# Moving the scaling and the sums of two weight groups in a fused state-space and mish kernel

## The chip, the cores and the metric

The kernel runs on one core of a Trainium2 chip. The core has five engines with an instruction queue each: PE (TensorE, matrix products), DVE (VectorE), ACT (ScalarE), POOL (GpSimd) and SP (SyncE, here only an issuer of DMAs). Each queue is worked off in order, and an instruction that waits for a semaphore holds up everything behind it on its queue. The metric is the device time of one execution in microseconds (us); less is better. Three executions of the kernel before took 611.64, 612.21 and 613.2 us, so the median is 612.21 us.

## The reference: what is computed

The input x has 2048 tokens of 1024 features. Each token is normalised, `xn = layernorm(x)`, and two layers are added to x:

```python
out = x + A(xn) + B(xn)
# A: a diagonal complex recurrence over the 2048 tokens
Bu  = xn @ B_bar.T                      # 1024 -> 1024 complex
h_t = Lam_bar * h_{t-1} + Bu_t          # one state per feature, token after token
y   = 2 * Re(h @ C.T) + xn * Dskip      # 1024 complex -> 1024
# B: a dense layer with the mish activation
u   = xn @ w1 + b1                      # 1024 -> 3584
act = u * tanh(softplus(u))
z   = act @ w2                          # 3584 -> 1024
```

## The kernel before, in words

The tokens go through in four blocks of 512 (`blk` 0 to 3). The code counts from zero, so "block 2" of the change is `blk == 1`, which the code calls `FAST`, and "weight groups six and seven" are the groups 5 and 6 below. A block has these stages on PE: the first layer of B (28 tiles of 128 of the 3584 columns, `first_tile`, weights of w1 through a ring of 7 slots), the projection into the states (B_bar), then the `tail`: the second layer of B (28 tiles, 8 PSUM banks as accumulators) and the projection out of the states (C), which adds into the same banks. While PE is in the tail's dense part, DVE runs the recurrence: `recur(blk, j)` for j = 0 to 7, two scans and four products and sums each. At the end `finish` adds the banks to x on DVE, a quarter of the tokens at a time, and ACT issues the stores.

From `blk` 1 on, the projection into the states is made with seven products of half size in place of eight, from sums of the weights and sums of xnT ("1" to "7" of pairs a to d in the orders `HEAD` and `WHOLE`; L882 are its matmuls; `evacuate` copies or adds what they leave in PSUM, on DVE for a and b, and for c and d on ACT with the additions on DVE). In `blk` 2 and 3 (`SPLIT`) the first layer of B is made in the same way (L952).

For that, the 1024 x 3584 matrix w1 must be turned into scaled 16-bit sums once, in seven groups of 512 columns, while blocks 0 and 1 run. For group i:

- `w_load(i)`: four DMAs on POOL's queue (L1026, 256 KB each) bring the group into SBUF. There are only three places: groups 0, 3 and 5 share one in the tile `hb`, groups 1, 4 and 6 share the other in `hb`, and group 2 lies in `act`. A load waits until the last sums of the group before it in its place have been stored.
- a power of two per group: for groups 3 to 6 from maxima taken in block 0; for groups 0 to 2 from `w_abs(i)` (a sum of absolute values, ACT, L1037), `w_row(1)` (POOL, two small DMAs through DRAM so that every partition sees every value, L1060 and L1063) and `w_exponent(1)` (seven small DVE instructions, L1071 to L1078).
- `w_scale(i)`: two ACT instructions (L1087) that scale the group in place, then three POOL DMAs (L1081) that store the raw units 1, 2 and 4 to the DRAM tensor `wsd`.
- `w_sums(i)`: four DVE instructions (L1102), which write units 5, 7, 6 and 3 over the group's own place, so that each but one waits for a store of `w_scale` to have landed; each is followed by one POOL store. With `later=True` the four are only put on the list `steps`, and the mark `k0` in an order, or `steps.pop(0)()`, takes the next one from it.

The places of all this are written by hand. In `blk` 1, `side(f)` puts work behind tile f of the first layer; `project_fast` walks through `WHOLE`, in which `v` is `w_scale`, `n` is `w_load`, `u` opens a unit of the tail (six dense matmuls), `r` is `rotate_in` on DVE; the loop over `recur` places the rest. Before the change: group 5 is scaled behind tile 20 and summed behind tile 26; group 6 is loaded behind tile 23, scaled at the head of the projection (`v6`) and summed at its four `k0`; groups 0 and 1 are loaded at the projection's end (`n0 n1`) and group 2 behind `recur(1)`; groups 0 to 2 are scaled behind `recur(6)`, and their twelve sums are steps in the first projection of `blk` 2.

Of the kernel before, what the change touches and what calls it, by code (L numbers as in the profile page):

```python
# [163 lines left out]
def build_kernel(nc, A_x, A_Lambda_re, A_Lambda_im, A_B_re, A_B_im, A_C_re, A_C_im,  # L164
# [16 lines left out]
    FAST = 1  # L181
# [1 line left out]
    SPLIT = range(2, NB)  # L183
    GROUPS = ((0, 7), (7, NPL), (NPL, NPL + 8), (NPL + 8, NF))
    HEAD = "a2 a1 b2 b1 a5 b5 a6 b6 a3 b3 a7 b7 c2 d2 a4 b4 c5 c1 r0 d5 d1 r1 c6 c3 d6"
    HEAD1 = "v6 " + HEAD.replace("a4 b4 c5 c1 r0 d5 d1 r1", "a4 k0 b4 c5 c1 k0 r0 d5 d1 k0 r1 k0")
    WHOLE = HEAD1 + " d3 c7 d7 u7 c4 r2 u5 d4 u6 u4 r3 n0 n1 r4 r5 r6 r7"
    LATE = (" a3 b3 a7 b7 c2 d2 a4 b4 c5 c1 d5 d1 c6 c3 d6"
            " d3 c7 w1 d7 w5 w2 c4 d4 w6 r0 x1 x5 x2 w7 w3 r1 x6 w4 y1 y5 y2 x7 x3 r2 y6 x4"
            " z1 z5 g2 z2 y7 y3 z6 y4 u0 z7 u2 z3 u1 z4 u7 g3 r3 r4 r5 r6 r7")  # L190
# [162 lines left out]
    ncs, _ = early("ncs", [P, NR], f32, 10752)  # L353
# [665 lines left out]
    def w_load(i):  # L1019
        sem = DmaSem(nc, "d_wraw%d" % i, nper=4)  # L1020
        for ci in range(2):
            for kh in range(2):
                dst, b_dst = w_unit(w_raw(i, ci, kh))
                f0 = (4 * i + 2 * ci) * P
                src = B_w1[kh * NH * P:(kh + 1) * NH * P, f0:f0 + 2 * P].rearrange("(k p) f -> p k f", p=P)
                PO.dma(lambda e, dst=dst, src=src: e.dma_start(dst.rearrange("p (k f) -> p k f", k=NH), src),  # L1026
                       sem, writes=b_dst)
# [56 lines left out]
    def w_scale(i):  # L1084
        for ci in range(2):
            t, b_t = w_half(i, ci)
            aop(lambda e, t=t: e.activation(t, t, AF.Copy, scale=wsm(2, i, i + 1)),  # L1087
                reads=b_t + [b_wsm[2][i]], writes=b_t)
        for n, ci, kh in ((1, 0, 0), (2, 0, 1), (4, 1, 1)):
            w_store(i, n, *w_unit(w_raw(i, ci, kh)))  # L1090

    steps = []

    def w_sums(i, later=False):
        (rl_, b_rl_), (rh_, b_rh_), (il_, b_il_), (ih_, b_ih_) = (w_unit(w_raw(i, ci, kh))
                                                                  for ci in range(2) for kh in range(2))
        for n, o, b_o, x, b_x, y, b_y, op in ((5, ih_, b_ih_, il_, b_il_, ih_, b_ih_, ALU.add),
                                              (7, il_, b_il_, rl_, b_rl_, il_, b_il_, ALU.subtract),
                                              (6, rl_, b_rl_, ih_.bitcast(f16), b_ih_, rl_, b_rl_, ALU.subtract),
                                              (3, rh_, b_rh_, rh_, b_rh_, rl_.bitcast(f16), b_rl_, ALU.subtract)):  # L1100
            def step(n=n, o=o, b_o=b_o, x=x, b_x=b_x, y=y, b_y=b_y, op=op):
                vop(lambda e: e.tensor_tensor(o.bitcast(f16), x, y, op=op), reads=b_x + b_y, writes=b_o)  # L1102
                w_store(i, n, o, b_o)

            steps.append(step)
        while steps and not later:
            steps.pop(0)()
# [282 lines left out]
    for blk in range(NB):  # L1390

        def side(f):
            if blk:
                at = (8, 10, 12, 15)
                if f in at:
                    ln_skip(blk, at.index(f))
                    if blk >= FAST:
                        sums_x(at.index(f))
                if blk == FAST:
                    if f == 1:  # L1400
                        rows_spread(1)
                    if f == 0:
                        scale_B(0, (1,))
                    if f < 3:
                        scale_B(f + 1)
                    if f in (3, 4, 17, 19):
                        sums_B((3, 4, 17, 19).index(f))
                    if f in (2, 14, 20):
                        w_scale((2, 14, 20).index(f) + 3)
                    if f in (6, 8, 10, 12):  # L1410
                        rows_C(f // 2 + 1)
                    if f == 12:
                        snaps_ready()
                    if f in (10, 19, 26):
                        w_sums((10, 19, 26).index(f) + 3)
                    if f in (15, 23):
                        w_load((f - 15) // 8 + 5)
                    if f == 27:
                        w_sums(6, True)
                return  # L1420
            if f == 2:
                turn_sines()
            if f == NR:
                aop(lambda e: e.activation(act[:, 0:NR, 0:2 * P], hraw[:, 0:NR, :], AF.Mish),
                    reads=b_hbf[0:4], writes=b_actf[0:NR])
            if f in (19, 27):
                for j in range(4):
                    table(j + (4 if f > 19 else 0))
            if f in (5, 6, 7, 8):
                coefficients(f - 5)  # L1430
            if f in (8, 9, 11, 12):
                ln_skip(0, (8, 9, 11, 12).index(f))
            if f in turns:
                transpose_B(turns.index(f))
            if f >= 26:
                transpose_C(f - 26)
            if f >= 4 * ROWS[0][0] and f % 4 < 2:
                w_most(f // 4, f % 4)
            if f in (23, 25, 26, 27):
                ln_stats_only(1, (23, 25, 26, 27).index(f))  # L1440
            if f == 26:
                w_row(0)

        for f in range(0 if blk in SPLIT else NF):
            first_tile(blk, f)
            side(f)

        near = 0 < blk < NB - 1
        out_stage = tail(blk, n_item[0] + (len(W_ITEMS) if blk in SPLIT else 0))
        open_unit = next(out_stage)  # L1450
        if blk in SPLIT:
            if near:
                for q in range(NQ):
                    load_x(PO, blk + 1, q)
            project_fast(blk, STEPS if near else SEVEN, open_unit)
        elif blk:
            project_fast(blk, WHOLE, open_unit)
        else:
            project_in()
        if near and blk not in SPLIT:  # L1460
            for q in range(NQ):
                next_stats(blk + 1, q)
            w_abs(0)
            w_abs(1)
        for j in range(NJ):
            if blk == 0 and j == NJ - 1:
                rows_scale(0)
            recur(blk, j)
            if near and j == (5 if blk in SPLIT else 1):
                next_root()  # L1470
                for q in range(NQ):
                    next_scale(blk + 1, q)
            if blk in SPLIT:
                if j == 1:
                    next(out_stage)
                if near and j == 1:
                    for q in range(NQ):
                        next_stats(blk + 1, q)
                if near and j == 5:
                    for q in range(NQ):  # L1480
                        transpose_dma(q)
                continue
            if blk:
                if j == 1:
                    next(out_stage)
                    w_load(2)
                    w_abs(2)
                    w_row(1)
                if j == 6:
                    w_exponent(1)  # L1490
                    for i in (0, 1, 2):
                        w_scale(i)
                continue
            if j == 0:
                ln_root()
                w_exponent(0)
                for q in range(NQ):
                    ln_scale(1, q)
                next(out_stage)
                for i in range(NHS):  # L1500
                    rows_load(i)
            scale_C(j)
            for i in {4: (0, 1, 2), 5: (3, 4, 5, 6), 6: (7, 8, 9, 10), 7: range(11, 16)}.get(j, ()):
                rows_size(i)
        if near:
            for q in range(NQ):
                ln_skip(blk + 1, q)
            for n in range(4):
                sums_x(n, VE)
        if blk < NB - 1:  # L1510
            carry()
        if blk == FAST:
            for i in (0, 1, 2):
                w_sums(i, True)
        if blk == FAST - 1:
            w_load(3)
            rows_scale(1)
            vop(lambda e: e.tensor_tensor(qi[:], qi[:], c("ss").unsqueeze(1).to_broadcast([P, 2, NJ]), op=ALU.mult),
                reads=[b_qi] + b_ss, writes=[b_qi])
            rows_spread(0)  # L1520
            scale_B(0, (0,))
            for j in range(4):
                rows_C(j)
            w_load(4)
        for _ in out_stage:
            pass
# [36 lines left out]
```

## Time and profile before

| what | value |
|---|---|
| profiled execution: time | 612.28 us |
| its span | 611.0 us |
| median of three executions | 612.21 us (611.64 to 613.2) |
| PE busy | 598.2 us, 98% of the span |
| DVE busy | 476.4 us, 78% |
| ACT busy | 278.4 us, 46% |
| POOL busy | 123.2 us, 20% |
| mean granted PE clock | 0.997 of full |

The span is what the profiler saw from the first to the last instruction; the time has 1.3 us more around it. "L1102" is line 1102 of the kernel before. A start such as 218.61 is in us from the start of the span. In a timeline a line gives start, length, engine, line, operation, what is written and read, how many instructions were merged, and in brackets how long the engine sat idle before it and what ended that. A matmul of 512 columns shows as 379 ns and one of 256 as 273 ns because neighbours overlap; from start to start they take 216 and 109 ns, so one product of eight half-size matmuls takes 0.874 us (eight products begin between 225.26 and 232.25). "PEclk" in a table of windows is the granted PE clock as a share of full speed.

### The profile page before, as it was taken

What the parts mean: (1) busy time and instruction counts of PE and PEld (TensorE: products, weight loads), DVE (VectorE), ACT (ScalarE), POOL (GpSimd) and SP (SyncE); (2) the same over time, 40 slices, a digit from 0 to 9 for tenths busy, and PEclk for the clock granted to TensorE, in tenths of its full rate; (3) what the DMA queues carried; (4) which work ended last, traced back from release to release, by engine and by line L of the source; (5) the groups of instructions that cost most, each with busy time, mean ns of one, the idle gap of its engine ahead of it and who ended that gap; (6) DMA issues with size and microseconds to landing.
All of it is one profiled execution on the core that took longest, in us unless ns stands there. A gap on an engine that the chain in (4) does not pass through costs nothing.

```text
span 611.0 us, 9307 instructions
## 1 busy us (share of the span) xinstructions
PE 598.2 (98%) x3583; PEld 349.2 (57%) x3583; DVE 476.4 (78%) x748; ACT 278.4 (46%) x367; POOL 123.2 (20%) x162
## 2 busy tenths in 40 slices
PE   9999999999999879999999999999999999999998
PEld 7644444444444457444448888644446888744444
DVE  6997899999789467989936877699943577689923
ACT  4749605489488432891706516570304615620000
POOL 2899200322338432500302200000000000000000
PEclk9999999999999989999999999999999999999999
DMA  9999998992999971969769917654666805754521
GB/s 235 318 228 278 205 178 230 268 352 50 267 362 337 342 260 71 280 202 220 254 201 375 375 41 239 208 205 138 182 198 240 281 15 167 248 206 142 165 73 69
DMA packets 109670, 132.95 MB, mean 218 GB/s; under 512 B 54346, under 2 KB 69322, under 8 KB 109626
## 3 DMA queue, kind: packets, MB, share of 16 engines
q1 hardware_dynamic: 97168, 95.77, 53.9%
q0 software_dynamic: 8768, 28.26, 14.0%
q10 hardware_dynamic: 3690, 8.34, 4.0%
q8 instruction: 28, 0.46, 0.3%
q14 instruction: 16, 0.13, 0.1%
HBM read 99.04 MB, written 21.24 MB: 197 GB/s over the span
## 4 chain that ended last, share of the span: by engine, by line
PE 70%; DVE 17%; DMA 7%; ACT 2%; issue 2%; POOL 1%; ACTq 0%; DVEq 0%; SPq 0%
PE ps L1193 37%; PE ps L952 10%; PE ps L882 9%; PE ps L818 6%; PE ps L1139 5%; DVE hT L1158 3%; DMA wsd<-hb 2%; DVE CT L789 2%; DVE CT L786 2%; DVE mt L1163 2%; ACT snaps L972 2%; DMA ring<-in_B_w_dram 1%; DMA scd<-sbf 1%; DMA hb<-in_B_w_dram 1%; DVE hb L1102 1%
## 5 line engine op out<-in xcount | busy, mean ns | idle before, releaser
L1193 PE MATMUL ps<-ring,act 128*128 128x512 bf16 x896 | 195.7, 379 | 0.4 <-DMA ring<-in_B_w_dram 0.3
L1193 PEld LDWEIGHTS ps<-ring,act 128*128 128x128 bf16 x896 | 87.6, 98 | 104.2 <-DMA ring<-in_B_w_dram 1.4
L972 ACT ACTIVATE snaps<-ps,par,cs 128x256 f32<-128x256 f32 x80 | 43.4, 563 | 99.0 <-PE ps L952 49.4
L818 PE MATMUL ps<-xnT,ring 128*128 128x512 bf16 x392 | 84.9, 379 | 0.0
L1193 PE MATMUL ps<-ring,hT 128*128 128x512 bf16 x378 | 82.1, 379 | 0.0
L818 PEld LDWEIGHTS ps<-xnT,ring 128*128 128x128 bf16 x392 | 38.3, 98 | 46.1
L1193 PEld LDWEIGHTS ps<-ring,hT 128*128 128x128 bf16 x378 | 36.9, 98 | 44.7
L1158 DVE TENSOR_TENSOR_SCAN hT<-cs,qi,hT 128x512 bf16<-128x512 f32 x48 | 58.9, 1269 | 0.0
L952 PE MATMUL ps<-TT,ring 128*128 128x256 f16 x448 | 55.8, 273 | 0.5 <-ACT snaps L972 0.5
L989 DVE SCALAR_TENSOR_TENSOR act<-ps,cs,snaps 128x512 bf16<-128x512 f32 x42 | 31.4, 750 | 31.2 <-PE ps L952 26.2
L952 PEld LDWEIGHTS ps<-TT,ring 128*128 128x128 f16 (+1 forms) x448 | 43.7, 98 | 6.9 <-issue 1.0
L952 PE MATMUL ps<-xnT,ring 128*128 128x256 bf16 x336 | 42.9, 273 | 0.0
L1163 DVE TENSOR_TENSOR mt<-hT,tab 128x1024 bf16<-128x1024 bf16 x64 | 41.4, 688 | 1.1
L1262 DVE TENSOR_TENSOR xx<-ps,xx 128x1024 bf16<-128x1024 f32 (+1 forms) x16 | 18.8, 1190 | 28.8 <-PE ps L1193 28.7
L826 ACT ACTIVATE act<-ps,par 128x512 bf16<-128x512 f32 (+1 forms) x56 | 33.6, 666 | 12.8 <-PE ps L818 10.9
L1087 ACT ACTIVATE hb<-hb,cs 128x2048 bf16<-128x2048 bf16 x12 | 23.3, 1995 | 32.3 <-DMA hb<-in_B_w_dram 16.7
L952 PEld LDWEIGHTS ps<-xnT,ring 128*128 128x128 bf16 (+1 forms) x336 | 32.9, 98 | 4.7
L841 ACT ACTIVATE act<-act 128x4096 bf16<-128x4096 bf16 (+2 forms) x8 | 25.5, 3189 | 19.0 <-DVE act L975 19.0
L1081 POOL DMA_DIRECT2D wsd<-hb x42 | 23.0, 550 | 49.3 <-DVE hb L1102 23.6
L848 DVE TENSOR_TENSOR mt<-hT,tab 128x1024 bf16<-128x1024 f16 x48 | 31.0, 687 | 0.4
L882 PE MATMUL ps<-TT,SS 128*128 128x256 f16 x192 | 24.9, 283 | 4.0 <-DVE snaps L897 4.0
L1102 DVE TENSOR_TENSOR hb<-hb 128x1024 f16<-128x1024 bf16 (+1 forms) x24 | 18.4, 767 | 13.4 <-DMA wsd<-hb 13.1
(178 smaller groups left out, 810.2 us busy)
## 6 DMA issues: line engine op xcount, KB each, us to landing
ring<-in_B_w_dram SPq DMA_DIRECT2D x84, 512.0 KB, 5.0
ring<-wsd SPq DMA_DIRECT2D x98, 256.0 KB, 4.1
ring<-ctd SPq DMA_DIRECT2D x24, 512.0 KB, 3.4
wsd<-hb POOLq DMA_DIRECT2D x42, 256.0 KB, 6.2
hb<-in_B_w_dram POOLq DMA_DIRECT2D x24, 256.0 KB, 5.9
ctd<-act ACTq DMA_DIRECT2D x8, 512.0 KB, 5.9
out_dram<-xx ACTq DMA_DIRECT2D x15, 256.0 KB, 3.4
xx<-in_A_x_dram POOLq DMA_DIRECT2D x12, 256.0 KB, 6.8
```

Of the source, the lines that this page charges most:

```text
L818: PE.mm(lambda e, k=k, w=w: e.matmul(ps[:, bank, :], lhsT=w, rhs=xnT[:, k, :], start=k == 0, stop=k == NK - 1), reads=[b_ring[s]] + b_xnT, ...
L826: aop(lambda e: e.activation(at[0][:, ts], ps[:, bank, ts], AF.Mish, bias=b1(f)), reads=[b_ps[bank], b_par], writes=[at[1]])
L841: aop(lambda e: e.activation(t, t, AF.Mish), reads=b, writes=b)
L848: vop(lambda e, s=s: e.tensor_tensor(mt[:, s, :, :], hT16[:, :, j, :], tab[:, s, j, :].unsqueeze(1).to_broadcast([P, 2, TB]), op=ALU.mult) ...
L882: PE.mm(lambda e, w=w, x=x, o=o, begin=begin, end=end: e.matmul(ps[:, bank, o:o + TH], lhsT=w, rhs=x, start=opens and begin, stop=end, ski ...
L952: PE.mm(lambda e, w=w, x=x, o=o, begin=begin, end=end: e.matmul(ps[:, bank, o:o + TH], lhsT=w, rhs=x, start=opens and begin, stop=end, ski ...
L972: aop(lambda e, o=o, p=p, j=j: e.activation(o, p, AF.Identity, scale=ig, bias=b1(f0 + j)), reads=[b_ps[b], b_par, b_ig], writes=b_dst)
L989: vop(lambda e: e.scalar_tensor_tensor(out=dst, in0=bank(b), scalar=ig, in1=src, op0=ALU.mult, op1=ALU.add), reads=[b_ps[b], b_snap[k], b_ ...
L1139: PE.mm(lambda e, j=j, ci=ci, k=k, bank=bank: e.matmul(ps[:, bank + ci, :], lhsT=BT[:, ci, j, k, :], rhs=xnT[:, k, :], start=k == 0, stop= ...
L1158: vop(lambda e, ci=ci, init=init: e.tensor_tensor_scan(out=hT[:, ci, j, :], data0=cj("r", j).to_broadcast([P, TB]), data1=hT[:, ci, j, :], ...
L1163: vop(lambda e, s=s: e.tensor_tensor(mt[:, s, :, :], hT[:, :, j, :], tab[:, s, j, :].unsqueeze(1).to_broadcast([P, 2, TB]), op=ALU.mult), ...
L1193: PE.mm(lambda e: e.matmul(ps[:, u, :], lhsT=lhsT, rhs=rhs, start=st_, stop=last), reads=reads, writes=[b_ps[u]], first=st_, last=last, te ...
```

## The change

Group 5 is no longer scaled and summed inside the first layer of `blk` 1: it is scaled at the head of the projection, behind ACT's last mish, and summed at the projection's four `k0`, the first of which moves one product later. Group 6 is loaded at the head of the projection behind group 5's raw stores, scaled behind d6 (ACT's last snapshot), and summed behind `recur(0)` and `recur(1)`, two sums each. The load of group 1, which needs group 6's place, moves behind them, its `w_abs` behind the next block's normalisation, and the exponents and scalings of groups 0 to 2 from behind `recur(6)` to behind `recur(7)`. PE's and SP's instructions and their order stay as they are, and the number of instructions on every engine too.

```diff
-    HEAD1 = "v6 " + HEAD.replace("a4 b4 c5 c1 r0 d5 d1 r1", "a4 k0 b4 c5 c1 k0 r0 d5 d1 k0 r1 k0")
-    WHOLE = HEAD1 + " d3 c7 d7 u7 c4 r2 u5 d4 u6 u4 r3 n0 n1 r4 r5 r6 r7"
+    HEAD1 = "v5 n6 " + HEAD.replace("a4 b4 c5 c1 r0 d5 d1 r1", "a4 b4 k0 c5 c1 k0 r0 d5 d1 k0 r1 k0")
+    WHOLE = HEAD1 + " v6 d3 c7 d7 u7 c4 r2 u5 d4 u6 u4 r3 n0 r4 r5 r6 r7"
...
-                    if f in (2, 14, 20):
-                        w_scale((2, 14, 20).index(f) + 3)
+                    if f in (2, 14):
+                        w_scale((2, 14).index(f) + 3)
...
-                    if f in (10, 19, 26):
-                        w_sums((10, 19, 26).index(f) + 3)
-                    if f in (15, 23):
-                        w_load((f - 15) // 8 + 5)
+                    if f in (10, 19):
+                        w_sums((10, 19).index(f) + 3)
+                    if f == 15:
+                        w_load(5)
                     if f == 27:
-                        w_sums(6, True)
+                        w_sums(5, True)
...
             w_abs(0)
-            w_abs(1)
+            w_sums(6, True)
         for j in range(NJ):
             if blk == 0 and j == NJ - 1:
                 rows_scale(0)
             recur(blk, j)
+            if blk == FAST and j < 2:
+                for _ in range(2):
+                    steps.pop(0)()
+                if j == 1:
+                    w_load(1)
...
                     w_load(2)
+                    w_abs(1)
                     w_abs(2)
                     w_row(1)
-                if j == 6:
+                if j == 7:
                     w_exponent(1)
                     for i in (0, 1, 2):
                         w_scale(i)
```

## The prediction, made before the result was known

> **What bounds the kernel now.** I read the page first, then who waits for whom on PE, then the windows and timelines of the two places where PE is not full.
>
> ```profile
> PE 598.2 (98%) x3583; PEld 349.2 (57%) x3583; DVE 476.4 (78%) x748; ACT 278.4 (46%) x367; POOL 123.2 (20%) x162
> ...
> PE ps L882 <- DVE snaps L897: 4.0, 1, 4.0
> PE ps L882 <- ACT act L826: 2.6, 2, 2.2
> PE ps L882 <- DVE hT L907: 1.3, 1, 1.3
> ```
>
> PE is busy for 98% of the span, so only what PE waits for, or loses in clock, can be won; what other engines do is worth nothing by itself. The three waits below the dots are all that PE has between 160 and 260 us, and they lie in one stage: the projection of `blk` 1. The timelines of PE, ACT, DVE and POOL there, and the windows behind them, say whose they are.
>
> ```profile
> 167.72 42.25 PE L818 MATMUL ps<-xnT,ring 128*128 128x512 bf16 x195
> 212.13 1.91 PE L882 MATMUL ps<-xnT,BT 128*128 128x256 bf16 x16 [2.16 <-ACT act L826]
> 214.44 1.91 PE L882 MATMUL ps<-xnT,BT 128*128 128x256 bf16 x16 [0.41 <-ACT act L826]
> 216.19 1.91 PE L882 MATMUL ps<-TT,SS 128*128 128x256 f16 x16
> 222.14 3.28 PE L882 MATMUL ps<-TT,SS 128*128 128x256 f16 x16 [4.05 <-DVE snaps L897]
> 225.26 1.91 PE L882 MATMUL ps<-xnT,SS 128*128 128x256 bf16 x16
> ...
> 207.52 3.90 ACT L1087 ACTIVATE hb<-hb,cs 128x2048 bf16<-128x2048 bf16 x2 [8.90 <-DMA hb<-in_B_w_dram]
> 211.32 4.14 ACT L826 ACTIVATE act<-ps,par 128x512 bf16<-128x512 f32 x7
> 223.25 3.90 ACT L1087 ACTIVATE hb<-hb,cs 128x2048 bf16<-128x2048 bf16 x2 [7.79 <-DMA hb<-in_B_w_dram]
> ...
> 218.61 2.87 DVE L1102 TENSOR_TENSOR hb<-hb 128x1024 f16<-128x1024 bf16 x4 [13.09 <-DMA wsd<-hb]
> ...
> 222.00:226.00 4.00, 3.86 (x23) 2.95 (x24) 3.93 (x8) 2.75 (x2) 0.78 (x2) 0.63 0.45 170
> ...
> 290.72 0.42 DVE L1168 TENSOR_TENSOR hT<-mt 128x512 bf16<-128x512 bf16 x1
> 291.06 0.66 DVE L1071 TENSOR_REDUCE cs<-wmx 128x3 f32<-128x384 f32 x1
> ...
> 312.63 1.23 DVE L1262 TENSOR_TENSOR xx<-ps,xx 128x1024 bf16<-128x1024 f32 x1 [6.18 <-PE ps L1193]
> ```
>
> ACT stands at 198.6 before group 5's scaling, because its load has not landed; behind it seven mishes queue up, PE runs through its eight banks and waits for the first of them. DVE stands from 205.5 before group 5's sums, because a raw store has not landed; behind it are the snapshots of a1 and b1, which free the banks that a6 and b6 write. After its idle time PE's granted clock is 0.63 in the window from 222 to 226. The last two rows are for later: DVE reaches the exponents with no wait, and has 6 us left before PE needs it again.
>
> **What the change takes away.** The first layer ends at 209.97 in the model of ends; its last matmul began at 209.59 and takes 0.216 from start to start, so the projection could begin at 209.81. Six products before a6 at 0.874 make 5.24, so a6 could begin at 215.05; it begins at 222.14: **7.09 us** of waiting (2.16 + 0.41 + 4.05, and 0.16 of overlap lost at each). Then a6 and b6 take 3.12 (225.26 less 222.14) where two products take 1.75: **1.37 us** of low clock. Together 8.46. With group 5 behind the last mish no ACT instruction waits in front of a mish, and DVE, idle from 205.5, takes a1's snapshot when a1 ends. It has 14 instructions of about 0.65 for the first 16 products of 0.874, so it keeps up. Both waits and the clock loss go: **-8.46**.
>
> **What is late next, step by step** (new times are old ones less 8.46 from a3 on, so c5 begins at 223.8 instead of 232.25).
>
> Group 5's scaling, 2 ACT instructions of 1.99: last mish until 210.8, scaling until 214.7 (load landed at 207.5). Behind it ACT has c5's snapshot, wanted at 224.7. Cost 0, covered by 10 us. Its third store (unit 4), which the first sum needs: in the old run DVE could go on 7.2 us after ACT's scaling ended (211.42 to 218.61), so now at 221.9. The first `k0` follows b4's cast, on DVE at 224.8. Cover 2.9; with the slowest of these stores (8.4 to landing, issued at 215.0) 223.4, still in time. The four sums cost what group 6's cost there before, DVE's time 2.7 either way, and the first now falls into 1.35 us in which DVE waited for a snapshot. PE's third wait, 1.3 us for c7's addition, comes from the DVE chain behind it, which does not change: it stays. Cost 0.
>
> Group 6's load, 4 POOL DMAs behind group 5's three stores: issue from 215.7, landing as before 11.8 after the end of group 5's scaling (211.4 to 223.25), so 226.5. Its scaling stands behind d6's snapshot, which ends at 230.95: cover 4.4. It holds ACT until 234.85; behind it is c4's cast, wanted at 236.4 (244.84 before), which PE's unit u4 waits for. Cover 1.5, cost 0; each us beyond would be a us of PE.
>
> Group 0's load (`n0`): POOL now holds it until group 5's last sum, at 232.8, is stored: about 240.5 instead of 243.23, landing near 249. `w_abs(0)` on ACT is reached at 250.7. Cost 0.
>
> Group 6's sums, 4 DVE instructions and 4 POOL stores behind two scans: +2.7 on DVE, but the wait of 2.4 before L551 goes, since `w_abs(1)` no longer stands before it on ACT. DVE ends `recur(7)` at about 287.4 (297.2 less 8.46, less the 1.7 of exponents now behind it, +0.3). PE needs j = 7 only in `finish`, from about 301. Cost 0.
>
> Groups 1 and 2, then the exponents: the long chain. Group 6's last sum at 260.1, its store landed near 266.5 (6.2 is the median); eight loads of 0.75 on POOL, the last until 272.5, landed near 279; `w_abs(1)` and `w_abs(2)` until 283.6; the two small DMAs took 11 us from the end of `w_abs(2)` (276.9) to about 288: now 294.6. DVE stands 7 us before L1071. From there to the end of the carry it needs 10.9 (306.5 less 291.06, without `recur(7)`'s 4.5): 305.5. `finish` wants DVE at 304.2, 306.8, 309.4 and 311.9, 1.23 each, so the first is 1.3 late and the third in time. The stores and PE's first product of `blk` 2 (from 311.7) see nothing. Behind L1076, ACT scales groups 0 to 2, six instructions, until 307.8, still before its stores of x; their nine POOL stores end at 309 and delay the next loads of x by 1 us. The sums of group 0 begin 3.5 us into `blk` 2, when its stores landed 8 us earlier. SP's order is the same; its loads of units of groups 5 and 6 come later than 300, and these stores land by 267. Cost 0, with 2.7 us of cover: PE is held only if the row lands after 297.3 (its landing + 10.9 + four finishes of 1.24 against 313.2).
>
> **Sum.** 612.28 of the profiled execution less 8.46 is **603.8** (span 602.5). The profiled execution is 0.07 above the median, so it stands for the median too.
>
> **A rule that speaks against the change.** Eight loads were issued from POOL in 5.95 us from 243.23 on, 0.744 each, while DVE was busy without a break; four took 2.99 at 212.24 while DVE stood idle. So busy DVE costs POOL's issue nothing here. The Trainium skill, "SBUF — State Buffer", section "SBUF: two separate sides", says that a two-port DVE instruction locks GpSimd out, so that it cannot write the descriptors of its DMAs; by that rule the loads moved between scans would be starved, and the sum would be that of rival 3; this trace so far disagrees.
>
> **Rivals.** (1) Part of it comes back at the projection: a store or load of groups 5 or 6 lands later than any seen, DVE waits at a `k0` or ACT before c4's cast. For: cover of only 2.9 and 1.5 us. Against: the slowest landing seen still fits. If the store takes 11.3, the longest landing of any on `wsd`, DVE is 1.5 to 2 late: 605.5. (2) The chain to the exponents is slow at every step: 8.4 for the store, 8.7 for the load, 5.4 twice for the rows. Then the row lands at 299.2, PE stands 1.9: 605.7. (3) Slower than before: POOL's issues wait behind scans. Each of the 14 between group 6's sums and the second small DMA then loses up to one scan, 1.27: the row lands at 312, PE stands 15 us, 619. It decides from a row at 305.8 on, 11 us later than worked out; speaking against it are the eight issues above. (4) The waits are not group 5's, and others take their places at once (mishes still late, snapshots still late): 611 to 612.5. Against: ACT's and DVE's rows name the load and the store.
>
> **Numbers.** Forecast 0.74; rivals 1 and 2 together 0.13; rival 3 0.05; rival 4 0.08, of which half within 0.3% (1.8 us, about what a measurement of this kernel can tell from no change) and half somewhat faster. A gain above 8.46 has no source but chip to chip differences of the size of the three executions (1.5 us). Range 602.4 to 607.3: the forecast, both bounds of rivals 1 and 2, and 1.5 beside. Faster by over 0.3%: 0.91; within: 0.04; slower: 0.05.
>
> **What will show it.** PE's first projection group starts at about 209.8 with no wait for ACT's mishes, a6 at about 215 at granted clock 1.00; the sums of group 5 begin near 224.8 without a wait for a DMA; the 1.3 before c4 is still there; DVE stands some 7 us before the exponents' first instruction, now behind `recur(7)`, and PE does not see it. Wrong it would be if PE waited at the start of `blk` 2, or DVE at the first `k0`.

## The result, and the profile after

The changed kernel takes 609.21 us (median of five executions, 607.7 to 609.85) against 613.2 us for the kernel before on the same chip (five executions, 611.64 to 613.86). The ratio is 0.9935 with a 95% interval of 0.9912 to 0.9958: 4.0 us faster, where 8.5 were forecast, and outside the forecast range (602.4 to 607.3). The profiled execution took 609.85 (span 608.6), 2.43 under the one before; it is the slowest of the five.

The first half of the prediction came out to about a tenth of a microsecond. These lines of the changed kernel answer to those shown of before: waits of PE over the whole span, then timelines of PE, ACT and DVE around the projection of `blk` 1.

```profile
PE ps L952 <- DVE xx L1262: 3.1, 1, 3.1
PE ps L1193 <- DMA ring<-in_B_w_dram: 1.1, 2, 0.7
...
195.67 14.19 PE L818 MATMUL ps<-xnT,ring 128*128 128x512 bf16 x64
209.70 3.66 PE L882 MATMUL ps<-xnT,BT 128*128 128x256 bf16 x32
...
235.18 1.05 PE L882 MATMUL ps<-TT,BT 128*128 128x256 f16 x8 [1.31 <-DVE hT L907]
...
210.48 3.88 ACT L1087 ACTIVATE hb<-hb,cs 128x2048 bf16<-128x2048 bf16 x2
...
224.48 0.68 DVE L1102 TENSOR_TENSOR hb<-hb 128x1024 f16<-128x1024 bf16 x1
```

PE goes from the first layer into the projection at 209.70, and the waits for ACT's mishes and for a6 are gone from the list. The granted clock stays at 1.00 from 208 to 233. These are lines of PE in the kernel before, at c4 and at the start of `blk` 2:

```profile
243.76 1.05 PE L882 MATMUL ps<-TT,BT 128*128 128x256 f16 x8 [1.32 <-DVE hT L907]
...
320.20 1.04 PE L952 MATMUL ps<-xnT,ring 128*128 128x256 bf16 x8
...
327.57 1.91 PE L952 MATMUL ps<-TT,ring 128*128 128x256 f16 x16 [0.23 <-ACT snaps L972]
```

The product c4, which began at 243.76, begins at 235.18: **8.58 us** won. The wait of 1.3 before c4 is still there. New on top of the list is a wait of 3.1 for DVE's `finish` (L1262) at the start of `blk` 2. The next lines are the timelines of ACT, POOL, DVE and PE of the changed kernel on the way there, and one of its windows, in which the last three columns are the granted clock, the share of the DMA engines and GB/s.

```profile
275.99 3.62 ACT L1037 ACTIVATE CT<-hb 128x4096 bf16<-128x4096 bf16 x1 [11.07 <-DMA hb<-in_B_w_dram]
286.54 3.62 ACT L1037 ACTIVATE CT<-act 128x4096 bf16<-128x4096 bf16 x1 [6.84 <-DMA act<-in_B_w_dram]
...
318.92 6.42 ACT L972 ACTIVATE snaps<-ps,par,cs 128x256 f32<-128x256 f32 x12 [3.40 <-DVE xx L1262]
...
265.46 2.23 POOL L1026 DMA_DIRECT2D hb<-in_B_w_dram  x3 [1.97 <-DMA wsd<-hb]
267.69 2.96 POOL L1026 DMA_DIRECT2D act<-in_B_w_dram  x4
290.54 0.56 POOL L1060 DMA_DIRECT2D wmd<-cs  x1 [19.89 <-ACT CT L1037]
...
286.78 0.42 DVE L1168 TENSOR_TENSOR hT<-mt 128x512 bf16<-128x512 bf16 x1
302.53 0.67 DVE L1071 TENSOR_REDUCE cs<-wmx 128x3 f32<-128x384 f32 x1 [15.34 <-DMA wmx<-wmd]
313.50 4.61 DVE L1262 TENSOR_TENSOR xx<-ps,xx 128x1024 bf16<-128x1024 f32 x4
...
314.86 1.03 PE L952 MATMUL ps<-xnT,ring 128*128 128x256 bf16 x8 [3.09 <-DVE xx L1262]
...
324.43 1.91 PE L952 MATMUL ps<-TT,ring 128*128 128x256 f16 x16 [0.76 <-ACT snaps L972]
...
315.50:318.60 3.10, 3.10 (x18) 2.21 (x17) 2.60 (x3) 0.01 (x1) 0.54 (x1) 0.55 1.02 378
```

Group 2's load is issued from 267.69 to 270.65 and `w_abs(2)` gets it at 286.54. The row of maxima lands at 302.5, DVE has stood 15.3 us before it, and its four `finish` instructions run from 313.50 instead of from 304. PE could have begun `blk` 2 at 311.6 (304.70 + 7.07, less the 0.16 of overlap) and begins at 314.86, and then runs at a granted clock of 0.55 for three microseconds.

The loss counted: from where PE could begin to its first product that waits for ACT's snapshots, the kernel before needs 7.37 us (320.20 to 327.57), the changed one 12.82 (311.61 to 324.43), so 5.45 of the 8.59 that had reached this place are lost. What sets this is the last of the four `finish`: it ends at 318.1, ACT's snapshots stand on ACT's queue behind the store that follows it, the first begins at 318.92, and PE's product comes 5.51 later. With load 2 first (below), where PE waits for no `finish` and the clock is full, that stretch is 5.52 long (312.78 to 318.30). So PE's wait of 3.1 and its low clock lie inside the 5.45 and add nothing to it. That leaves 3.14. Another 0.9 goes at the next opening of dense units, where PE waits 1.1 for ring loads instead of 0.3; 2.2 are left there, and the two profiled spans differ by 2.4 at their ends.

### The profile page after: what moved, and what is told of

The parts are those of the page before. It is cut to its first block, busy times and chain, and to the rows that moved or that the text cites. A ratio compares the mean times of both kernels' runs of the same rounds, so it can differ in the third digit from the quotient of the medians.

```text
span 608.6 us, 9262 instructions
## 1 busy us (share of the span) xinstructions
PE 595.7 (98%) x3541; PEld 348.8 (57%) x3583; DVE 475.4 (78%) x748; ACT 278.5 (46%) x367; POOL 122.8 (20%) x162
## 4 chain that ended last, share of the span: by engine, by line
PE 78%; DVE 9%; DMA 5%; issue 5%; ACT 2%; POOL 1%; SPq 1%; ACTq 0%; DVEq 0%; POOLq 0%
PE ps L1193 37%; PE ps L818 14%; PE ps L952 11%; PE ps L882 10%; PE ps L1139 5%; DMA ring<-in_B_w_dram 2%; DVE mt L848 2%; ACT snaps L972 2%; DMA wmd<-cs 1%; PE ps L638 1%; DVE xx L1262 1%; DVE hT L907 1%; DVE hT L1158 1%; DMA wmx<-wmd 1%; DMA wsd<-hb 1%
## 5 line engine op out<-in xcount | busy, mean ns | idle before, releaser
L1262 DVE TENSOR_TENSOR xx<-ps,xx 128x1024 bf16<-128x1024 f32 (+1 forms) x16 | 18.5, 1186 | 18.7 <-PE ps L1193 18.6
L897 DVE COPY snaps<-ps 128x512 f32<-128x512 f32 x30 | 19.9, 685 | 12.9 <-PE ps L882 12.8
L907 DVE TENSOR_TENSOR hT<-ps,snaps 128x512 f16<-128x512 f32 x36 | 24.4, 689 | 5.6 <-PE ps L882 3.7
```

Of the source, the lines that this page charges most:

```text
L907: vop(lambda e: e.tensor_tensor(dst, bank(b), src, op=ALU.add), reads=[b_ps[b], b_src], writes=b_hT[ci][j0:j0 + 2])
```

## The experiments

Theory 1: PE pays for the late row of maxima. Group 2's load stands on POOL behind group 6's stores, then moves beside the DMA transposes of the next block's xn; the row comes late, and DVE, which waits for it ahead of `finish`, is late with it. Theory 2, the rival: the loss comes from the DMA traffic of that stretch as such (C rows or transposes late), and DVE's wait only happens to lie beside it. Each time below is a median; a ratio is to the kernel before on the same chip, with its 95% interval, and a difference in us is worked out from the ratio.

**Group 2's load first.** POOL's order around `recur(1)` is changed, and the order of two `w_abs`; group 6's last two sums move with their stores, behind the normalisation's two small instructions on DVE:

```diff
-            if blk == FAST and j < 2:
+            if blk == FAST and j == 0:
                 for _ in range(2):
                     steps.pop(0)()
-                if j == 1:
-                    w_load(1)
...
                     w_load(2)
-                    w_abs(1)
+                    for _ in range(2):
+                        steps.pop(0)()
+                    w_load(1)
                     w_abs(2)
+                    w_abs(1)
                     w_row(1)
```

> Edit: the changed kernel, but behind recur(1) the load of group 2 is issued from POOL ahead of group 6's last two sums' stores and of group 1's load, and w_abs(2) ahead of w_abs(1). Theory 1 (the row of maxima is late because group 2's load stands on POOL behind group 6's stores and then moves beside the transposes of the next block): load 2 is issued from about 255 and landed by 265, the row lands near 292, DVE is through before finish wants it at 304.2, PE starts blk 2 with no wait at full clock: 8.5 us under the kernel before, 4.5 under the changed one. Theory 2 (the loss at the start of blk 2 is due to DMA traffic as such, the C rows or the transposes being late, and not to the row): the same bytes move in the same stretch, so it stays within 1 us of the changed kernel, 3 to 4.5 us under the kernel before.

Measured: 603.55 us against 613.05, ratio 0.9852 (0.9837 to 0.9867): 9.1 us under the kernel before. Timelines of ACT, POOL, DVE and PE:

```profile
264.85 3.62 ACT L1037 ACTIVATE CT<-act 128x4096 bf16<-128x4096 bf16 x1 [1.93 <-DMA act<-in_B_w_dram]
277.23 3.62 ACT L1037 ACTIVATE CT<-hb 128x4096 bf16<-128x4096 bf16 x1 [8.68 <-DMA hb<-in_B_w_dram]
...
312.78 6.49 ACT L972 ACTIVATE snaps<-ps,par,cs 128x256 f32<-128x256 f32 x12 [9.47 <-DVE xx L1262]
...
254.59 2.98 POOL L1026 DMA_DIRECT2D act<-in_B_w_dram  x4
...
290.32 0.67 DVE L1071 TENSOR_REDUCE cs<-wmx 128x3 f32<-128x384 f32 x1 [3.77 <-DMA wmx<-wmd]
303.35 1.23 DVE L1262 TENSOR_TENSOR xx<-ps,xx 128x1024 bf16<-128x1024 f32 x1 [1.97 <-PE ps L1193]
...
310.92 1.04 PE L952 MATMUL ps<-xnT,ring 128*128 128x256 bf16 x8
...
318.30 1.91 PE L952 MATMUL ps<-TT,ring 128*128 128x256 f16 x16 [0.23 <-ACT snaps L972]
```

Load 2 is in use at 264.85, the row lands at 290.3, DVE waits for PE at `finish` and not the other way, and PE enters `blk` 2 with no wait. Theory 1 expected 8.5, theory 2 at most 4.5. The ratio of this version is 0.0083 below that of the changed kernel, 5 us. No version below is faster, and two of them cannot be told from it (0.9853 and 0.9858).

**No wait for the row.** The two small DMAs and everything before them stay, DVE does not use their result:

```diff
-        vop(lambda e: e.tensor_reduce(out=m, in_=src.rearrange("p (q j) -> p j q", j=n),
-                                      axis=mybir.AxisListType.X, op=ALU.max), reads=b_wmx[h], writes=b_m)
+        if h == 1:
+            vop(lambda e: e.tensor_scalar(m, wsm(1, 3, 6), 1.0, None, op0=ALU.mult), reads=b_wsm[1][3:6], writes=b_m)
+        else:
+            vop(lambda e: e.tensor_reduce(...))
```

> Edit: the changed kernel, but the exponents of groups 0 to 2 are worked out from the maxima of groups 3 to 5, which DVE has had since block 0 (the loads, w_abs and the two small DMAs of the row all stay, only their result is not used: this part of the computation, the own maxima of groups 0 to 2, is left out). So DVE waits for nothing at the exponents. Theory 1: DVE goes on at 287.4, is through by 298, PE starts blk 2 at once: 8.5 us under the kernel before. Theory 2: PE still waits or slows at the start of blk 2 with the DMA traffic unchanged: 4 us under the kernel before.

Measured: 604.53 against 613.05, ratio 0.9863 (0.985 to 0.9877), 8.4 us less. The loads were as late as in the changed kernel (`w_abs(2)` began at 287.5), the DMA share from 262 to 292 was 1.05 as there, and PE began `blk` 2 with no wait:

```profile
311.75 1.04 PE L952 MATMUL ps<-xnT,ring 128*128 128x256 bf16 x8
```

So the loss comes by the wait for the row. What the late traffic may cost PE beside it is at most the 0.7 us between this version and the one with load 2 first, and the intervals of the two overlap. Theory 2 falls.

**The wait behind the carry, and behind recur(6).** Two places for the same wait. In the first, `w_exponent(1)` and the three `w_scale` are moved from behind `recur(7)` to behind `carry()`; in the second, to where they were before the change (this edit is shown):

```diff
-                if j == 7:
+                if j == 6:
                     w_exponent(1)
                     for i in (0, 1, 2):
                         w_scale(i)
```

> Edit: the changed kernel with the exponents and the scaling of groups 0 to 2 behind the carry, so that DVE does the skip terms, the sums of x and the carry before it waits for the row. Theory 1: the row lands at 302.5 as in the changed kernel, DVE is ready for the first finish at 304.2, so PE sees no wait for DVE; but ACT scales from 304 to 315.6 and its first snapshot of blk 2 comes at 316.3 where 313.6 would be free: about 2.7 us of the 8.5 are lost, so 5.8 us under the kernel before and 1.5 to 2 under the changed one. Theory 2: no change against the changed kernel (4 us under the kernel before).

> Edit: the changed kernel with one part undone: the exponents and the scaling of groups 0 to 2 behind recur(6) again, as before the change. Theory 1: the row lands near 302.5 all the same, now recur(7), 4.5 us, stands behind the wait too, and everything up to finish comes 4.5 us later: about 4.5 us slower than the changed kernel, within 1 us of the kernel before. Theory 2 (DVE's wait for the row is not what PE pays): within 1 us of the changed kernel, since PE wants the last scan only from about 301 on.

Measured: behind the carry 606.9, ratio 0.9907 (0.9891 to 0.9923), 5.7 us under the kernel before; behind `recur(6)` 613.31, ratio 1.001 (0.9995 to 1.0026), nothing left of the gain. In the first, DVE waits until 302.65 with all other work done and is at `finish` at 304.31; now ACT's scalings end at 315.6 and its first snapshot comes at 315.54, so PE waits 2.5 for snapshots in all, against 0.5 in the kernel with load 2 first, near the 2.7 worked out (its profiled execution of 609.1 us also waits 2.4 for units of `wsd`, so not all of its loss is the snapshots). In the second, PE waits for the results of the last `recur` themselves:

```profile
PE ps L1193 <- DVE hT L1166: 4.5, 1, 4.5
```

Against load 2 first, one row that lands near 302 costs about 3 us (behind the carry), 5 (the changed kernel) or 10 (behind `recur(6)`), by what stands behind the wait.

**Why the load was late.** Theory C: the transposes on SP stretch it. Theory D: eight loads in a row are slow by themselves. In the first of two kernels only SP's transposes move (`f1 = 21` in place of 17 in `blk` 1), which puts two of SP's plain loads of C ahead of them. In the second it is POOL's order, load 2 ahead of load 1 and both behind group 6's last store, and with it the order of the two `w_abs`.

> Edit: the changed kernel, but in blk 1 SP issues the four transposes of the next block's xn behind dense tiles 21 to 27 in place of 17 to 23, about 7 us later; POOL's order is untouched. Theory C (the transposes, which move through the same 16 DMA engines, are what stretches group 2's load from some 7 to 16 us): the eight loads of 262 to 271 land before or soon after the transposes begin at about 274, load 2 by about 278, w_abs(2) ends near 284, the row lands near 297, PE loses at most 1 us at the start of blk 2: 7.5 to 8.5 us under the kernel before. Theory D (eight loads in a row on POOL are slow by themselves): load 2 lands at 286 as in the changed kernel, the row at 302, and the time stays within 1 us of the changed kernel's.

> Edit: the changed kernel with the loads of groups 1 and 2 exchanged on POOL's queue, both still behind group 6's last store, and w_abs(2) ahead of w_abs(1). Load 2 need not wait for the landing of these stores, so it goes at 261 to 264 and load 1 at 264 to 267, the last of the eight 3.5 us sooner than in the changed kernel and just ahead of the first transpose at 267. Theory C: most of the eight pass before the transposes, load 1 lands near 279, the row near 293: no wait at blk 2, about 8.5 us under the kernel before. Theory D: eight loads take 23 us from the first to the last landing, so load 1 lands near 284, the row near 299.5: PE loses 2 us, 6 to 6.5 us under the kernel before.

Measured: transposes later 604.41 against 612.78, ratio 0.9858 (0.984 to 0.9875), 8.7 us less, with the row at 295.1; loads exchanged 604.19, ratio 0.9853 (0.9832 to 0.9874), 9.0 less. First the DMA issues of the changed kernel between 262 and 292 (size, median from issue to landing), then windows of it; then the same of the kernel with the later transposes.

```profile
act<-in_B_w_dram POOLq DMA_DIRECT2D x4, 256.0 KB, 13.9
xnT<-xn SPq DMA_TRANSPOSE x4, 11.4
...
271.00:275.00 4.00, 4.00 (x20) 1.84 (x19) 3.93 (x7) 0.00 (x0) 0.00 (x0) 1.00 1.16 140
275.00:279.00 4.00, 3.95 (x19) 1.78 (x19) 3.93 (x6) 3.01 (x1) 0.00 (x0) 1.00 1.25 121
```

```profile
act<-in_B_w_dram POOLq DMA_DIRECT2D x4, 256.0 KB, 7.1
xnT<-xn SPq DMA_TRANSPOSE x4, 6.0
...
271.00:275.00 4.00, 4.00 (x21) 1.80 (x19) 3.93 (x6) 0.00 (x0) 0.00 (x0) 1.00 0.94 295
275.00:279.00 4.00, 4.00 (x20) 1.82 (x19) 3.93 (x7) 3.71 (x2) 0.00 (x0) 1.00 1.37 335
```

With the same eight loads issued at nearly the same times, but the transposes from 274.8 on, load 2 lands in 7.1 instead of 13.9 us (longest 11.1 instead of 16.6), and a transpose in 6.0 instead of 11.4. From 271 to 279 the changed kernel, with loads and transposes in flight, reads as fully busy on its DMA engines and moves 140 and 121 GB/s; the version with later transposes moves 295 before the first of them, and 335 beside it and the last loads; over 271 to 283 it is 145 against 277 GB/s. So moving the transposes is enough to bring the loads back in time: theory C holds for the changed kernel. Theory D is out, since eight loads in a row landed soon enough.

Transposes beside loads are not slow in every case, though. In the exchanged version the last of the eight loads was issued by 267.96 instead of 270.65, about when the first transpose went out (267.87); its loads landed in 4.6 to 9.5 us, `w_abs(1)` began at 276.8 and the row came at 290.4. With load 2 first, only group 1's four loads (issued from 266.05 to 269.43) met the transposes (from 266.7 on), and they landed in at most 8.5. The long landings came only where loads issued behind the first transpose met four others still in flight; which of the two counts for how much is not shown. What inside the DMA engines makes them slow each other is not shown.

The Trainium skill, "DMA: Bandwidth & Descriptors", section "Issuing engines are not separate DMA queues", says that transfers from all issuers run on the same 16 engines and interleave. These rows agree: SP's transposes and POOL's loads slow each other in the changed kernel although they are issued from different queues.

**One stall alone.** Into the kernel before, only group 5's sums are moved out of DVE's queue behind tile 26, and the projection gets eight marks:

```diff
-"a4 k0 b4 c5 c1 k0 r0 d5 d1 k0 r1 k0"
+"a4 k0 k0 b4 c5 c1 k0 k0 r0 d5 d1 k0 k0 r1 k0 k0"
...
+                    if f == 26:
+                        w_sums(5, True)
```

> Edit: the kernel before with one part of the change alone: group 5's sums are taken from behind tile 26 and put on the list, and the projection has eight marks in place of four, two at each place, for the sums of groups 5 and 6. ACT's scalings, all loads and the tail stay as they were. Expected if the two stalls are separate and as sized in the prediction: the 4.05 of waiting for DVE (with its lost overlap 4.2) and the 1.37 of low clock go, ACT's 2.9 stays; the four further sums stand in the DVE chain that PE waits for ahead of c4, three of them not covered, about 1.9, so PE's wait there grows from 1.3 to about 3.2. Sum: 3.7 us under the kernel before. If the waits were one and the same (rival 4 of the prediction): within 1 us of the kernel before.

Measured: 609.87 against 612.78, ratio 0.9945 (0.9925 to 0.9966), 3.4 us less (3.7 expected). Timeline of PE:

```profile
212.01 1.91 PE L882 MATMUL ps<-xnT,BT 128*128 128x256 bf16 x16 [1.57 <-ACT act L826]
...
240.23 1.89 PE L882 MATMUL ps<-TT,BT 128*128 128x256 f16 x8 [3.41 <-DVE hT L907]
```

ACT's waits stay and DVE's at a6 is gone: they are two stalls. The wait before c4 grows from 1.3 to 3.4 (3.2 expected), which is a reason for the change to take group 6's four sums out of the projection when it puts group 5's in. In this execution (610.9 us) c4 begins 3.53 earlier than before (240.23 against 243.76), but behind that wait the clock was 0.50 from 240 to 243, which the expectation had left out, and at PE's next product of the projection only 2.19 are left (243.75 against 245.94). So it is in part luck that the measured 3.4 comes so near to 3.7; its interval is 2.1 to 4.6.

**Control.** The changed kernel again, beside the last three.

> The changed kernel once more beside these, as a control: 4 us under the kernel before, the row of maxima landing near 302 by the trace.

Measured: 609.37 against 612.78, ratio 0.9929 (0.991 to 0.9948), 4.4 us less, with the row at 302.8 and PE's wait of 3.0 at `blk` 2.

## Why the prediction was right and wrong

- *What the change takes away, -8.46:* right; 8.58 at c4. Both waits and the low clock went, and with the stall on DVE alone taken away 3.53 were won at c4, where 3.7 were expected.
- *Group 5's and group 6's scaling and sums, cost 0:* right. Scaling ends at 214.36 (214.7 predicted), the first sum begins at 224.48 (224.8) without a wait for its store, group 6's scaling ends at 234.6, before c4's cast at 236.3.
- *Group 0's load, group 6's sums behind the scans, DVE at the end of `recur(7)` at 287.4:* right; 287.2. Group 0's load went out at 235.7 and not at 240.5, which cost nothing.
- *The long chain to the exponents, cost 0 with 2.7 of cover:* **this step failed.** The mechanism and the place were named, and the threshold too: PE is held if the row lands after 297.3, and the rows at 290.3, 290.4 and 295.1 of the experiments held nothing. What was mis-sized is the landing of the loads: the sum has 6.5 us from the last issue to the last landing (272.5 to 279), the run had 15.9 (270.65 to 286.5), although the issue came 1.9 sooner than forecast. So `w_abs(2)` ended at 290.3 instead of 283.6, the two small DMAs took 12.3 instead of 11, and the row came at 302.5 and not at 294.6. For a row at 302.5 the prediction's own formula gives a stall of 5.2; 5.45 was lost. This agreement is not luck: the formula goes by the end of the fourth `finish`, and ACT's snapshots start only behind that end.
- The reason for the wrong term: landing times were taken from the run before, where load 2 had moved from 251 to 265, ahead of the transposes that began at 276. The change puts it at 267.7, just behind the first transpose, which itself moved to 267.4. The prediction counted every queue that a step is moved past, but not what else would be on the DMA engines at the new time. The trace had the warning: from 275 to 279 in the run before, beside the first transpose, the DMA share was 1.10 at 162 GB/s.
- *Rival 2, slow at every step, 605.7:* the right rival with too small a bound. Its worst load, 8.7, was the longest seen in the run before; with transposes beside it, 16.6.
- *Rival 3 and the rule on DVE and POOL's descriptors:* rival 3 was not seen. With DVE busy in scans the four loads from 267.69 were issued in 2.96 us, 0.74 each, as in the run before, and it was not DVE that made them land late: with DVE just as busy (3.93 of each 4 us from 267 to 279 in both) and the transposes later they landed in 7.1. The rule that the prediction took from the Trainium skill, "SBUF — State Buffer", section "SBUF: two separate sides", is about two-port DVE instructions; no trace here shows whether the scans and products of this stretch are such, so these runs do not test it.
- *A range of 602.4 to 607.3:* too narrow at the top, since its upper end came from that bound. The 0.9 at the ring loads was not in the sum either.

## What to carry to other kernels

A transfer that is moved in time must be priced by what shares the DMA engines at its new time, not by its landing time at the old one; here four DMA transposes in the midst of eight loads took the landing of load 2 from 7.1 to 13.9 us, while four loads beside them were hardly slower. A wait in an in-order queue costs what stands behind it: the same late row cost about 3, 5 or 10 us by where the waiting instruction stood. When a change frees a stall and pays with a longer chain elsewhere, look first at which link of that chain can be issued earlier: here one load ahead of two stores brought back the 5 us that were lost.

## What the runs showed of the hardware

With four DMA transposes in the midst of eight loads of POOL (the changed kernel, 271 to 279) the DMA engines read as fully busy (shares of 1.16 and 1.25) and moved 140 and 121 GB/s; load 2 landed in 13.9 us and a transpose in 11.4 (medians), against 5.2 for a transpose in the run before. With the same loads and the transposes about 7 us later it was 295 and 335 GB/s, 7.1 and 6.0 us. Four loads beside the transposes (load 2 first) landed in at most 8.5 us.

PE's granted clock fell to about half for some 3 us after waits of 3.0 us (the control, 0.50 from 316 to 319), 3.1 (changed kernel, 0.55 from 315.5 to 318.6), 3.4 (0.50 from 240 to 243 in the kernel with one stall alone), 4.05 (before) and 4.5 (0.50 from 307 to 310 with the wait behind `recur(6)`), but not after the 2.16 us at 212 in the run before. No run has a wait between 2.2 and 3.0. The low clock cost 1.37 us in the kernel before and 1.34 in the one with one stall alone (3.52 instead of 2.18 from c4 to the next product of the projection); in the changed kernel it cost nothing more, since PE waits for ACT's snapshots at 324.43 all the same. The Trainium skill, "TensorE: Matmul & The Clock Gate", section "Part 1: The HAM clock gate (the "warmup" mystery)", tells of a window of about 3.4 us in which an idle PE is throttled and a busy one released. These rows agree in size, with the shortest wait that halved the clock a little below that figure.
